# Pairs 4 and 5 of an attention and MLP kernel: output turned by transposing transfers, in a new recorded order

## The chip, the cores and the metric

The kernel runs on one core of one Trainium2 chip. The metric is the device time of one execution in microseconds, the median over runs. A core has five engines that run at the same time, each with its own queue of instructions: PE (TensorE, matmuls), DVE (VectorE), ACT (ScalarE), POOL (GpSimd) and SP (SyncE, which here only issues transfers). They wait for each other through semaphores.

## The reference

`q`, `k`, `v` have 4 batches, 8 heads, 768 positions and 64 values. Attention is block-sparse and causal: the mean of each block of 64 keys is compared with each query, and a query attends to the three blocks with the highest score and to its own block. The result, 3072 rows of 512 values, goes through an MLP.

```python
k_rep = k.reshape(B, H, n_blocks, block, D).mean(axis=3)
gate_scores = np.where(causal, q @ k_rep, -1e9)
sel = top3(gate_scores) | own_block
scores = np.where(sel & causal_positions, q @ k.T / 8, -1e9)
x = (softmax(scores) @ v)          # to 3072 x 512
out = gelu_tanh(x @ w_in) @ w_out  # 512 x 2048, 2048 x 512
```

## The kernel before

**Tiling.** The unit of attention is a pair of heads, `p` = 0 to 15; batch `b` is `p // 4` (`HP` = 4). For each pair, k and q are loaded and turned so that the head dimension lies on partitions, key block sums are taken, a gate matmul (L679) gives block scores, DVE picks the three best (L695 to L716), and the mask is turned on PE (L748, pairs below 8) or by a transposing transfer (L755). Then come the score matmuls (L855 for pairs 0 to 3, L1038 later), the exponential on ACT (L874, L1051), the causal cut on POOL (L900, L1065), the product with v (L923, L1077) and the normalisation on DVE (L941 and L942, L960 and L961), which writes `xn`. The MLP follows per batch: `x @ w_in` with gelu (L1114, L1126; a seven-product form at L1203) and the product with `w_out` (L1314, L1364, L1413), then stores.

**Loads.** `load_0` (L412) brings pair 0 in halves, k by SP and q by ACT (L420). `load` (L366) brings the rest by SP: plain for pairs 0 to 3 (L386), which PE then turns (L537 for k, L540 for q), and in pieces that DVE can turn in 32x32 blocks for pairs 4 to 15 (L392, L556). For pairs 0 and 1 (`KSUM`) the turning matmul of k also gives block sums. `load_w` (L442) brings `w_in` and `w_out` by POOL's queue (L452). Both kernels have these plain loads and key sums.

**From `xn` to the MLP's input `xT`.** `turn_out` (L964) turns the output of a pair. One way, `ot_e`, takes six 128x128 transposes on PE (L980) into a PSUM bank, and a copy on DVE or ACT (L359 and L355 in `copy`) to SBUF. The other, `ot_dma`, is one transposing transfer that SP issues (L985).

**What sets the order.** The builder makes some 1960 operations, each with an emitter. `Plan.run` emits them in a recorded global order, a list of numbers (`ORDER`), with a recorded choice of buffer for each (`BUFFER`) and of engine for operations that several engines can do (`ENGINE`). Each engine's queue is this order restricted to the engine. There is no scheduler at build time. The order before was recorded for the kernel before. Dummy matmuls (L1516) are part of it: they fill PE in the first microseconds and in places later; there are 34.

Of the kernel before, what the change touches and what calls it, by code (L numbers as in the profile page):

```python
# [227 lines left out]
def kernel(  # L228
# [16 lines left out]
    HP = H // 2  # L245
# [720 lines left out]
    def turn_out(p, norms, base):  # L966
        b, hp = divmod(p, HP)
# [610 lines left out]
    for p in range(HP, NPAIR):  # L1578
# [3 lines left out]
        b, hp = divmod(p, HP)  # L1582
# [36 lines left out]
```

## Time and profile before

| what | value |
|---|---|
| median of 3 runs | 251.66 us (251.35 to 251.76) |
| profiled execution, own time | 251.91 us |
| its span in the profile | 250.2 us (1.71 us lie around it) |
| busy: PE, DVE, ACT, POOL | 243.9, 188.3, 174.7, 85.2 us |
| L980 transposes on PE | 54, of 219 ns mean |
| L985 transposing transfers | 7 |

A row of a timeline gives the start, the length from first start to last end, the engine, the line, what is written and read, and how many instructions are run together in the row; in brackets stands the idle time before it and what ended it. Matmuls overlap in the pipeline: the time that one holds PE is the distance to the next start, not its length.

### The profile page before, as it was taken

The page shows a single profiled execution, that of the slowest core. Times are in us where ns is not written, and L with a number is a line of the kernel's source. Part 1 is how long each engine was busy: PE and PEld are TensorE (multiplying, and loading weights), DVE is VectorE, ACT ScalarE, POOL GpSimd, SP SyncE. Part 2 cuts the span into 40 slices and gives each one's busy share as a digit, 9 for nine tenths or more (in the row PEclk, how much of TensorE's full clock was granted, in tenths as well). Part 3 has the DMA queues.
Part 4 walks back from the last instruction along what each step waited for, and adds up shares of the span by engine and source line. Part 5 has one row for each costly group of instructions (what it writes and reads, how often), then busy time and mean ns, then how long its engine had stood idle before and what let it go on. Part 6 is the DMA issues. An engine that isn't in the chain of part 4 may idle for free.

```text
span 250.2 us, 6424 instructions
## 1 busy us (share of the span) xinstructions
PE 243.9 (97%) x2480; PEld 170.2 (68%) x2480; DVE 188.3 (75%) x541; ACT 174.7 (70%) x220; POOL 85.2 (34%) x166
## 2 busy tenths in 40 slices
PE   8899999999999999999999999999999999999993
PEld 6767676554556566665778887656877877666882
DVE  2799671034989999999999987998878584687953
ACT  0778896553699999668999873676999937657300
POOL 8853970001245655342156644500245600000000
PEclk9999999999999999999999999999999999999999
DMA  8999599998999998997999999550310350010023
GB/s 160 218 196 195 86 213 189 213 170 138 158 132 161 150 122 130 158 198 176 145 219 204 160 174 159 132 162 19 65 45 4 63 159 2 15 71 0 3 109 142
DMA packets 130927, 32.61 MB, mean 130 GB/s; under 512 B 124529, under 2 KB 126929, under 8 KB 130897
## 3 DMA queue, kind: packets, MB, share of 16 engines
q1 hardware_dynamic: 126160, 27.62, 64.1%
q0 software_dynamic: 3136, 4.19, 9.9%
q10 hardware_dynamic: 1600, 0.39, 0.8%
q8 instruction: 19, 0.31, 0.6%
q14 instruction: 12, 0.09, 0.1%
HBM read 27.26 MB, written 6.29 MB: 134 GB/s over the span
## 4 chain that ended last, share of the span: by engine, by line
PE 80%; DMA 8%; SPq 6%; POOL 3%; issue 1%; DVE 0%; POOLq 0%
PE wide L1114 24%; PE bank L1364 22%; PE wide L1038 11%; PE bank L1314 9%; PE bank L1077 6%; SPq L386 6%; PE wide L1203 6%; DMA w_out<-in_moe_w_out_dram 5%; DMA TS<-in_v_dram 2%; PE bank L679 2%; POOL ats L900 2%; DMA G<-in_q_dram 1%; PE bank L980 1%; POOL v L357 1%; POOL w_in L452 1%
## 5 line engine op out<-in xcount | busy, mean ns | idle before, releaser
L1114 PE MATMUL wide<-xT,w_in 128*128 128x384 f16 x416 | 74.6, 326 | 0.0
L1051 ACT ACTIVATE ats<-wide 128x896 f16<-128x896 f32 x72 | 62.1, 915 | 4.9 <-PE wide L1038 3.3
L1126 ACT ACTIVATE G<-wide 128x768 f16<-128x768 f32 x52 | 41.8, 809 | 29.3 <-PE wide L1114 29.1
L1114 PEld LDWEIGHTS <-w_in 128*128 128x128 f16 x416 | 39.8, 98 | 26.7 <-issue 1.3
L1065 POOL TENSOR_SCALAR_AFFINE_SELECT ats<-ats 128x256 f16<-128x256 f16 x72 | 32.0, 460 | 58.1 <-ACT ats L1051 57.7
L1038 PE MATMUL wide<-qT,kT 76*128 76x512 f16 (+3 forms) x192 | 39.0, 305 | 0.0
L556 DVE STREAM_TRANSPOSE s<-sd 128x768 f32<-128x768 f32 x24 | 23.1, 969 | 14.9 <-DMA sd<-in_k_dram 13.1
L1364 PE MATMUL bank<-w_out,G 128*128 128x256 f16 x216 | 32.9, 272 | 0.0
L1364 PEld LDWEIGHTS <-G 128*128 128x128 f16 x288 | 26.9, 98 | 5.8
L1413 DVE TENSOR_TENSOR osb<-bank,osb 128x512 f32<-128x512 f32 (+1 forms) x38 | 22.2, 594 | 9.1 <-PE bank L1364 8.4
L1314 PE MATMUL bank<-w_out,G 128*128 128x512 f16 x96 | 28.8, 379 | 0.1
L1077 PEld LDWEIGHTS <-ats 128*128 128x128 f16 x504 | 22.4, 98 | 3.8 <-POOL ats L1065 0.2
L1077 PE MATMUL bank<-v,ats 128*128 128x65 f16 x504 | 24.4, 194 | 0.0
L1038 PEld LDWEIGHTS <-kT 76*128 76x128 f16 x192 | 17.2, 97 | 9.8 <-issue 0.5
L874 ACT ACTIVATE ats<-wide 128x1024 f16<-128x1024 f32 (+3 forms) x24 | 20.9, 916 | 3.5 <-PE wide L855 3.3
L1364 PEld LDWEIGHTS <-XS 128*128 128x128 f16 x216 | 20.1, 97 | 4.2
L357 POOL CAST kT<-s 64x768 f16<-64x768 f32 x20 | 17.1, 867 | 16.5 <-DVE s L556 16.1
L1364 PE MATMUL bank<-TS,XS 128*128 128x256 f16 x144 | 22.3, 272 | 0.0
L357 POOL CAST v<-vsd 128x768 f16<-128x768 f32 x13 | 10.9, 840 | 30.8 <-DMA vsd<-in_v_dram 30.8
L961 DVE TENSOR_TENSOR xn<-bank,zr 128x384 f16<-128x384 f32 x24 | 13.4, 557 | 0.8
L711 DVE MAX8 sel<-sel 128x8 f32<-128x12 f32 x160 | 13.3, 157 | 0.6
L355 ACT CAST qT<-s 64x768 f16<-64x768 f32 x16 | 13.2, 828 | 0.2
(118 smaller groups left out, 347.3 us busy)
## 6 DMA issues: line engine op xcount, KB each, us to landing
out_dram<-osb SPq DMA_DIRECT2D x23, 256.0 KB
vsd<-in_v_dram SPq DMA_DIRECT2D x26, 192.0 KB
sd<-in_k_dram SPq DMA_DIRECT2D x48, 96.0 KB
sd<-in_q_dram SPq DMA_DIRECT2D x48, 96.0 KB
w_in<-in_moe_w_in_dram POOLq DMA_DIRECT2D x2, 1024.0 KB, 10.8
w_out<-in_moe_w_out_dram POOLq DMA_DIRECT2D x2, 1024.0 KB, 14.9
G<-in_q_dram SPq DMA_DIRECT2D x4, 192.0 KB
G<-in_k_dram SPq DMA_DIRECT2D x4, 192.0 KB
```

Of the source, the lines that this page charges most:

```text
L357: nc.gpsimd.tensor_copy(out=out, in_=in_)
L556: nc.vector.transpose(out=T[key + "T32", p], in_=T[key, p].rearrange("p t j -> p (t j)"))
L874: nc.scalar.activation(out=T["at", u][:, :, 0:n], in_=plan.buf[("st",) + u].rearrange("p (h w) -> p h w", h=2)[:, :, 0:n], func=AF.Exp, bi ...
L1038: nc.tensor.matmul(st[:, x:e], kT16[i][h][0:76, s0:s0 + 128], qT16[i][h][0:76, s0 + (x - cb):s0 + (e - cb)], start=True, stop=True)
L1051: nc.scalar.activation(out=T["at", u][:, 0:n], in_=plan.buf[("st",) + u][:, 0:n], func=AF.Exp, bias=0.0, scale=SCALE)
L1065: nc.gpsimd.affine_select(out=dg, in_=dg, compare_op=ALU.is_ge, fill=0.0, base=0, pattern=[[0, 2], [1, 128]], channel_multiplier=-1)
L1077: nc.tensor.matmul(pvv[:, qc, 0:65], at[:, cb + (qc - jc) * 128: cb + (qc - jc + 1) * 128], v16[i][:, jc, h, :], start=(gi == 0 and jc == ...
L1114: nc.tensor.matmul(hps[:, 512 * e:512 * e + HALF], w_in16[:, ci, (2 * j + e) * 128: (2 * j + e + 1) * 128], T["xT", b][:, ci, HALF * h:HAL ...
L1126: nc.scalar.activation(out=G[:, :, h, j, :], in_=plan.buf["hps", b, j, h].rearrange("p (e w) -> p e w", e=2)[:, :, 0:HALF], func=AF.Gelu_a ...
L1314: nc.tensor.matmul(plan.buf["ops", b, ti], G[:, f % 2, 2 * ti // NC, f // 2, ti % (NC // 2) * 128:ti % (NC // 2) * 128 + 128], w_out16[:, ...
L1364: nc.tensor.matmul(dst[:, HD * h:HD * h + HD], FACT[m][0][:, j, t * 128:(t + 1) * 128], FACT[m][1][:, j, :], start=(clear and j == 0), sto ...
L1413: nc.vector.tensor_tensor(out=dst(), in0=src(), in1=other(), op=ALU.add)
```

## The change

One condition, and all three recorded lists:

```diff
-        if p >= HP + 2 and hp != HP - 1:
+        if p >= HP and hp != HP - 1:
             go = add({SP: 1.3}, ot_dma, norms, -50)
...
-    0, 1890, 6, 9, 1891, 1892, 1893, 1894, 1895, 15, 12, 1896, 1897, 1898,
...
+    1, 1892, 2, 1893, 1894, 1895, 6, 15, 1896, 1897, 9, 1898, 1899, 1900,
+    195, 12, 1901, 1902, 1903, 1904, 1905, 1906, 1907, 62, 64, 71, 22, 72,
...
```

By the condition, pairs 4 and 5 now take `ot_dma` as pairs 6, 8, 9, 10, 12, 13 and 14 did. `ORDER`, `BUFFER` and `ENGINE` are new throughout. Counted in the programs: L980 goes from 54 matmuls (and as many weight loads) to 42, L985 from 7 transfers to 9, copies of `xT` on ACT from 3 to 1, on DVE they stay 7; the number of all other operations is the same. Some twenty casts and copies change their engine among DVE, ACT and POOL. At the start, the first two of ACT's four loads of pair 0's q are the second half of the positions, and the last two the first half; before it was the other way round. ACT's first table load moves from its first copy (L355) to L821, ahead of it. The last of the 34 dummy matmuls moves behind all other matmuls.

More of the change, by code (lines that the diff above doesn't have):

```diff
@@ L21 @@
 ORDER = [
[128 rows of a table removed]
-BUFFER = [
[23 rows of a table removed]
[128 rows of a table added]
+BUFFER = [
[23 rows of a table added]
 ENGINE = {
     "ACT": [
[4 rows of a table removed]
[4 rows of a table added]
     "POOL": [
-        586, 587, 646, 647, 707, 708, 972, 973, 1035, 1036, 1097, 1098,
-        1159, 1160, 1425, 1489, 1550, 1551, 1612, 1613]}
+        338, 587, 588, 648, 649, 709, 710, 974, 975, 1037, 1038, 1099, 1100,
+        1161, 1162, 1427, 1428, 1490, 1491, 1552, 1553, 1614, 1615]}
 class Op:
```

307 rows, old and new, of tables (BUFFER, ENGINE, ORDER) are left out of this document.

## The prediction

> **What bounds the kernel now.** I read the page first: busy times, the chain that ended last, and the granted clock.
>
> ```profile
> span 250.2 us, 6424 instructions
> PE 243.9 (97%) x2480; PEld 170.2 (68%) x2480; DVE 188.3 (75%) x541; ACT 174.7 (70%) x220; POOL 85.2 (34%) x166
> PEclk9999999999999999999999999999999999999999
> PE 80%; DMA 8%; SPq 6%; POOL 3%; issue 1%; DVE 0%; POOLq 0%
> ```
>
> TensorE is busy for 243.9 of 250.2 us, at full clock, and four fifths of the last chain are its own. Busy time is an average, so the next view is the table of stretches (columns: stretch, its length, then busy us of PE, weight loads, DVE, ACT, POOL).
>
> ```profile
> 0.00:10.00 10.00, 8.36 (x71) 6.31 (x73) 4.14 (x31) 3.65 (x7) 8.09 (x28) 1.00 1.02 182
> 10.00:20.00 10.00, 9.50 (x144) 6.84 (x140) 9.24 (x38) 7.62 (x12) 6.73 (x15) 1.00 1.17 206
> 20.00:30.00 10.00, 10.00 (x190) 7.54 (x184) 8.85 (x40) 9.45 (x12) 5.98 (x11) 1.00 0.68 118
> 30.00:40.00 10.00, 9.78 (x166) 7.56 (x163) 5.33 (x14) 8.07 (x11) 5.83 (x10) 1.00 1.13 211
> 40.00:50.00 10.00, 9.91 (x62) 5.70 (x61) 0.36 (x1) 5.14 (x7) 0.00 (x0) 1.00 1.31 200
> 90.00:100.00 10.00, 10.00 (x119) 6.47 (x116) 9.80 (x20) 9.83 (x13) 6.54 (x13) 1.00 1.00 121
> ```
>
> PE has nothing to fill but the first 10 us (1.64 idle), 0.5 in the next ten, 0.3 around 40. In 90 to 100 it never stops, though DVE and ACT are almost as full there: the late rivals lie in that stretch. What PE waited for most, over the whole span (us in total, times, longest):
>
> ```profile
> PE bank L1516 <- DVE bmask L284: 1.1, 1, 1.1
> PE bank L748 <- DVE madd L716: 0.5, 2, 0.3
> PE bank L540 <- DMA G<-in_q_dram: 0.4, 1, 0.4
> ```
>
> So the kernel is a stream of matmuls with a short ramp and a short tail. The time moves by what leaves that stream, and by what happens to the ramp.
>
> **The change, part by part.**
>
> *Twelve transposes leave PE.* Pairs 4 and 5 no longer go through six L980 transposes each.
>
> ```profile
> 96.41 0.50 PE L980 MATMUL bank<-ident,xn 128*128 128x128 f16 x6
> 96.74 0.38 PE L1314 MATMUL bank<-w_out,G 128*128 128x512 f16 x1
> ```
>
> Matmuls are pipelined, so I take starts, not busy times: six transposes hold the stream from 96.41 to 96.74, 0.33 us. Two pairs: **−0.67 us**, with PE full on both sides.
>
> *One filler leaves the path.* The program before has 34 dummy matmuls (L1516), the last of them in the tail's stream; the new order puts that one behind all real work. A filler in the stream costs what these starts are apart:
>
> ```profile
> 28.63 0.28 PE L1516 MATMUL bank<-XS 128*128 128x256 f16 x1
> 28.75 0.44 PE L748 MATMUL bank<-ident,madd 128*128 128x128 f16 x5
> ```
>
> **−0.12 us.**
>
> *Two copies leave DVE and ACT*, those that emptied the transposes' bank:
>
> ```profile
> 87.71 0.55 DVE L359 COPY xT<-bank 128x768 f16<-128x768 f16 x1
> 97.22 1.61 ACT L355 COPY xT<-bank 128x768 f16<-128x768 f16 x2
> ```
>
> That is 0.55 us of DVE and half of 1.61 of ACT. The planner also moves some twenty casts and copies between DVE, ACT and POOL. None of this is on the chain (DVE 0% of it), so I count zero; it is cover for the waits below. Its gain is bounded by zero, as PE has no idle time there to give back.
>
> *Two transposing transfers enter SP's queue* (L985, seven to nine).
>
> ```profile
> L985 SPq DMA_TRANSPOSE xT<-xn x7: 1211/1239/2051, 92.8 to 199.0; - x7
> 88.17 2.75 SPq L392 DMA_DIRECT2D sd<-in_q_dram  x4
> 92.80 2.05 SPq L985 DMA_TRANSPOSE xT<-xn  x1
> 94.90 1.71 SPq L392 DMA_DIRECT2D sd<-in_k_dram  x3
> 85.05 0.56 DVE L961 TENSOR_TENSOR xn<-bank,zr 128x384 f16<-128x384 f32 x1
> 95.87 0.49 PE L1114 MATMUL wide<-xT,w_in 128*128 128x384 f16 x2
> 98.05 2.11 PE L1114 MATMUL wide<-xT,w_in 128*128 128x384 f16 x12
> ```
>
> Each holds SP for about 1.24 us, 2.48 together. They stand ahead of pair 6's, where SP sat from 90.92 to 92.80 for pair 6's normalised output, 1.88 us. So about 0.6 us of later loads remains. Their first consumers (L1114 of batch 1, pair 4 and then 5) stand at 95.87 before, and in the order of the new program at about the same place. Pair 5's output is finished on DVE at 85.6 (85.05 + 0.56), pair 4's earlier; a transfer issued at 88 to 90 has six microseconds. Pair 6's own, whose issue ran from 92.80 to 94.85, feeds the third of the twelve L1114 from 98.05 (about 98.5) without a wait, so four suffice. Cost 0, and if the cover goes, PE stalls by the lateness (a rival below). The Trainium skill, page "VectorE: DVE Perf Modes", section "Rules for kernel authors", advises the opposite choice: TensorE for a 128×128 transpose whose result may land in PSUM, the crossbar DMA otherwise. By that rule the −0.67 would not be worth the latency; the rows here say that PE, not latency, is scarce in this stretch.
>
> *The order at the start is different, and that costs.* In the program before ACT issues pair 0's q as first half, then second half (L420). In the new program the second half is issued first, while PE's order still needs the first half first (turn k, turn q's first half, q's second half, filler, gate).
>
> ```profile
> 0.81 2.15 ACTq L420 DMA_DIRECT2D G<-in_q_dram  x4
> 0.81 2.86 DMA G<-in_q_dram
> 5.21 0.49 PE L540 MATMUL bank<-identk,G 128*128 128x128 f32 x3
> 6.35 0.32 PE L679 MATMUL bank<-s,ksb 128*32 128x64 f32 x8 [0.21 <-DVE s L359]
> 7.59 0.52 PE L540 MATMUL bank<-identk,G 128*128 128x128 f32 x3
> G<-in_q_dram ACTq DMA_DIRECT2D x4, 96.0 KB
> G<-in_k_dram SPq DMA_DIRECT2D x4, 96.0 KB
> ```
>
> The first issued transfer has landed by 3.67 (0.81 + 2.86). When the third and fourth do, no row says. Earliest: by the issue spacing alone (2.15 / 4), two places later, 3.67 + 1.1 = 4.8. Latest: 7.59, where the second half's turn ran without a wait. Between them: eight transfers of 96 KB, of k and q, run together. The first ten microseconds carry 1820 KB, all of it after some 2 us, so 228 KB per us while data flow; the six or seven left after 3.67 take 2.6 to 3.0 us: 6.3 to 6.7. I take 6.7, so the turn goes from 5.21 to about 6.8, **+1.6 us** at the first gate.
>
> How much reaches the end of the ramp? PE cannot catch up, since it is full from 20 us; but PE is not what sets the ramp. The gates' chain on DVE does, busy 9.24 and 8.85 of ten: 1.9 us of idle time, part of it waits that shift along with PE. The exponential's table load (1.28 us, in front of ACT's first copy before) comes earlier in the new order, and q's second half is there at once. Bounds: 0 (all regained in DVE's gaps) and 1.6 (none). I take the middle, **+0.8 us** at the first expert matmul. Part of that is given back in a known place:
>
> ```profile
> 33.54 12.43 DMA w_out<-in_moe_w_out_dram
> 38.95 1.79 PE L1114 MATMUL wide<-xT,w_in 128*128 128x384 f16 x10
> 40.57 0.33 PE L980 MATMUL bank<-ident,xn 128*128 128x128 f16 x3
> 40.87 5.05 PE L1114 MATMUL wide<-xT,w_in 128*128 128x384 f16 x30
> 46.01 0.38 PE L1314 MATMUL bank<-w_out,G 128*128 128x512 f16 x1
> ```
>
> w_out lands at 45.97. Ten L1114 matmuls take 1.62 in the stream (38.95 to 40.57), thirty so 4.86; L1314 came 5.14 after the first of the thirty: 0.28 of waiting, less a few hundredths, which a PE that arrives 0.8 late doesn't have: **−0.27**. Net start: +0.5, bounds −0.3 and +1.3.
>
> *The tail* (PE's last matmul, an addition on DVE, the last store) has the same shape and shifts as a whole.
>
> **Sum**: −0.67 − 0.12 + 0.8 − 0.27 = −0.26 us. The profiled execution took 251.91 us (span 250.2 and 1.71 around it), which gives 251.65; it stands 0.25 above the median of the runs shown, 251.66, so for a median I forecast **251.4 us**. That is 0.1% off; about 0.2%, or 0.5 us, is what a measurement can tell from no change here.
>
> **Rivals.**
>
> *The ramp absorbs the late half.* Then the stream keeps its −0.79, and the w_out wait, if it goes too, adds 0.27: −0.8 to −1.06, **250.8 us**. For it: DVE's 1.9 us of gaps, and the table load out of the way. Against it: the gates form one chain, in which those gaps are mostly waits for PE.
>
> *DVE waits for loads that the new transfers hold back (slower).* Place: the 32x32 transposes (L556) of pair 9's q at about 98 us, and pair 15's k at about 153 (places in the new order, counted in DVE's work).
>
> ```profile
> 108.76 0.98 DVE L556 STREAM_TRANSPOSE s<-sd 128x768 f32<-128x768 f32 x1 [0.29 <-DMA sd<-in_k_dram]
> ```
>
> Before, one load already came 0.29 late. SP is 0.6 later in the new order, so such a wait is 0.9, and two of them 1.8 at most. DVE has 0.2 us spare in 90 to 100, and its delay reaches PE through the next gate's mask. With one to one and a half of these on PE: −0.26 + 1.3 = +1.04, **252.7 us**. It decides once those loads are issued less than about 3.2 us ahead of DVE's turn. Against it: DVE has 0.55 us less to do, and PE holds other matmuls to run meanwhile.
>
> *The transposed outputs come late.* If pair 4's transfer is issued with pair 6's at 92.8 instead of at 88, it lands behind its consumer, and PE stalls by about 1 us: −0.26 + 1.0, 252.4. The new SP order speaks against it.
>
> *The clock falls in the ramp.* PE would stand for about 1.7 us before the late turn. The granted clock is 1.00 in the first row, which holds 1.64 us of idle time in all, so I expect no fall. If it fell, at the doubled spacing of the first fillers for some 1.7 us, that would be 253.1. The Trainium skill, page "TensorE: Matmul & The Clock Gate", Part 1, puts the fall behind an idle window of about 3.4 us; by it, too, this gap is too short.
>
> **How the numbers follow.** Forecast case 0.42 (−0.65 to +0.3 us), ramp absorbed 0.25, DVE late 0.22, outputs late 0.07, clock 0.04. Faster by over 0.2%: the second and 0.08 of the first, 0.33. Within: 0.34 of the first, 0.02 of the fourth, 0.36. Slower: the rest, 0.31. The range leaves out the clock, the outer half of the absorbed case and the dearest DVE waits: 250.7 to 252.8.
>
> **What would show it.** 42 L980 matmuls and nine L985 transfers, the first two at 88 to 91 us. The first q turn near 6.8 and the first L679 near 8.0 instead of 6.35. The first L1114 about 0.8 later than 35.85 and no gap before the first L1314. PE without waits from 50 on: if a wait for a mask or for xT stands there, the slower rivals hold; if the first L1114 starts no later than before, the faster one.

## The result and the profile after

The changed kernel takes **253.86 us** (253.27 to 254.32) against 251.71 us (251.35 to 251.98): 1.0085 times as long, interval 1.006 to 1.011, 2.15 us more. The prediction was 251.4 us, inside 250.7 to 252.8; the time lies above. The profiled execution of the changed kernel took 253.96 us.

First the page: busy times and the chain that ended last.

```profile
span 252.2 us, 6405 instructions
PE 245.9 (98%) x2468; PEld 171.3 (68%) x2468; DVE 191.9 (76%) x538; ACT 173.7 (69%) x218; POOL 88.3 (35%) x169
PEclk9999999999999999999999999999999999999999
PE 89%; DVE 4%; ACT 3%; DMA 2%; issue 1%; POOL 1%; ACTq 1%; DVEq 0%; POOLq 0%
```

There are twelve matmuls fewer, and yet PE is "busy" for 2 us longer. That is the first sign: matmuls that run slowly count as busy. The row of the granted clock shows 9 in every slice of both kernels and doesn't tell; the spacing of the matmuls does. PE at the start, the kernel before and then the changed one:

```profile
4.46 0.92 PE L537 MATMUL bank<-identk,G 128*128 128x130 f32 x6
...
6.60 0.94 PE L537 MATMUL bank<-identk,G 128*128 128x130 f32 x6
```

```profile
4.46 1.56 PE L537 MATMUL bank<-identk,G 128*128 128x130 f32 x6
6.75 1.51 PE L540 MATMUL bank<-identk,G 128*128 128x128 f32 x6 [0.73 <-DMA G<-in_q_dram]
...
8.40 0.44 PE L679 MATMUL bank<-s,ksb 128*32 128x64 f32 x8
8.77 1.61 PE L537 MATMUL bank<-identk,G 128*128 128x130 f32 x6
10.22 0.38 PE L1516 MATMUL bank<-XS 128*128 128x256 f16 x2
```

Six L537 take 0.92 us before and 1.56 to 1.61 after, at 4.46 and still at 8.77. The trace's record of the clock says the same: full from 4.62 us before, from 10.19 after. The first turn of q comes at 6.75 (I had said 6.8), the first gate at 8.40 instead of 6.35.

What that makes of the expert stage, in the timeline of PE: the first L1314 stood at 46.01 before, the first L1114 at 35.85.

```profile
35.85 1.78 PE L1114 MATMUL wide<-xT,w_in 128*128 128x384 f16 x10
```

After:

```profile
38.25 0.81 PE L1114 MATMUL wide<-xT,w_in 128*128 128x384 f16 x4
...
47.94 0.59 PE L1314 MATMUL bank<-w_out,G 128*128 128x512 f16 x2
...
245.82 2.57 PE L1364 MATMUL bank<-w_out,G 128*128 128x256 f16 x22
```

The last row ends at 248.39; before, the last run of L1364 ended at 246.30:

```profile
243.52 2.78 PE L1364 MATMUL bank<-w_out,G 128*128 128x256 f16 x24
```

So PE is 2.40 us late at the first L1114, 1.93 at the first L1314 and 2.09 at the end. Between the last two the stream is 0.79 us shorter (transposes and dummy), so 0.95 us of new waiting has come in there. These rows of PE show the larger part of it:

```profile
88.12 0.93 PE L1038 MATMUL wide<-qT,kT 76*128 76x512 f16 x6
89.15 0.45 PE L748 MATMUL bank<-ident,madd 128*128 128x128 f16 x5
...
97.05 0.59 PE L1077 MATMUL bank<-v,ats 128*128 128x65 f16 x14
97.86 0.61 PE L1077 MATMUL bank<-v,ats 128*128 128x65 f16 x14 [0.22 <-POOL ats L1065]
```

The mask of pair 7 starts 0.27 us after its place in the stream (six L1038 take 0.76), and two groups of v products are 0.81 us apart where fourteen of them take 0.43 in the stream: 0.38. The rest, some 0.3, are small gaps at a gate near 71 us and in the last batch.

The transfers hold nobody up. SP's queue:

```profile
L985 SPq DMA_TRANSPOSE xT<-xn x9: 1211/1214/2265, 89.1 to 201.2; - x9
```

```profile
89.08 3.46 SPq L985 DMA_TRANSPOSE xT<-xn  x2
```

Both are issued from 89.08 on. Two take 3.46 us where one holds SP for 1.21, so SP waits about 1 us between them: pair 5's output is ready on DVE at 91.31 here, not at 85.6 as in the kernel before. No L1114 waits for xT. There is no wait of DVE for q's or k's pieces from 60 us on either.

### The profile page after: what moved, and what is told of

It is laid out like the page before. It is cut to its first block, busy times and chain, and to the rows that moved or that the text cites. A ratio compares the mean times of both kernels' runs of the same rounds, so it can differ in the third digit from the quotient of the medians.

```text
span 252.2 us, 6405 instructions
## 1 busy us (share of the span) xinstructions
PE 245.9 (98%) x2468; PEld 171.3 (68%) x2468; DVE 191.9 (76%) x538; ACT 173.7 (69%) x218; POOL 88.3 (35%) x169
## 3 DMA queue, kind: packets, MB, share of 16 engines
q0 software_dynamic: 3136, 4.19, 10.3%
## 4 chain that ended last, share of the span: by engine, by line
PE 89%; DVE 4%; ACT 3%; DMA 2%; issue 1%; POOL 1%; ACTq 1%; DVEq 0%; POOLq 0%
PE wide L1114 27%; PE bank L1364 22%; PE wide L1038 10%; PE bank L1314 7%; PE wide L1203 6%; PE bank L1077 5%; PE wide L855 3%; ACT ats L1051 2%; PE bank L679 2%; PE bank L923 2%; DMA G<-in_q_dram 2%; PE bank L540 1%; PE bank L537 1%; PE bank L980 1%; PE bank L1516 1%; PE bank L748 1%
## 5 line engine op out<-in xcount | busy, mean ns | idle before, releaser
L1114 PE MATMUL wide<-xT,w_in 128*128 128x384 f16 x416 | 75.2, 326 | 0.0
L1051 ACT ACTIVATE ats<-wide 128x896 f16<-128x896 f32 x72 | 62.9, 915 | 4.8 <-PE wide L1038 3.2
L1114 PEld LDWEIGHTS <-w_in 128*128 128x128 f16 x416 | 39.9, 98 | 26.4 <-issue 1.0
L1038 PE MATMUL wide<-qT,kT 76*128 76x512 f16 (+3 forms) x192 | 39.1, 305 | 0.0
L357 POOL CAST kT<-s 64x768 f16<-64x768 f32 x23 | 19.6, 856 | 38.8 <-DVE s L556 38.1
L1364 PE MATMUL bank<-w_out,G 128*128 128x256 f16 x216 | 32.7, 272 | 0.0
L1364 PEld LDWEIGHTS <-G 128*128 128x128 f16 x288 | 27.0, 98 | 5.9
L1314 PE MATMUL bank<-w_out,G 128*128 128x512 f16 x96 | 28.7, 379 | 0.0
L1077 PE MATMUL bank<-v,ats 128*128 128x65 f16 x504 | 25.1, 194 | 0.2 <-POOL ats L1065 0.2
L1038 PEld LDWEIGHTS <-kT 76*128 76x128 f16 x192 | 17.0, 97 | 10.3 <-issue 0.5
L1364 PEld LDWEIGHTS <-XS 128*128 128x128 f16 x216 | 20.0, 97 | 5.4 <-issue 0.2
L1364 PE MATMUL bank<-TS,XS 128*128 128x256 f16 x144 | 23.6, 272 | 0.0
L357 POOL CAST v<-vsd 128x768 f16<-128x768 f32 x13 | 11.9, 919 | 15.7 <-issue 8.2
L355 ACT CAST qT<-s 64x768 f16<-64x768 f32 x18 | 14.9, 827 | 0.3
```

The lines of the kernel that those rows point to most:

```text
L357: nc.gpsimd.tensor_copy(out=out, in_=in_)
L1038: nc.tensor.matmul(st[:, x:e], kT16[i][h][0:76, s0:s0 + 128], qT16[i][h][0:76, s0 + (x - cb):s0 + (e - cb)], start=True, stop=True)
L1051: nc.scalar.activation(out=T["at", u][:, 0:n], in_=plan.buf[("st",) + u][:, 0:n], func=AF.Exp, bias=0.0, scale=SCALE)
L1077: nc.tensor.matmul(pvv[:, qc, 0:65], at[:, cb + (qc - jc) * 128: cb + (qc - jc + 1) * 128], v16[i][:, jc, h, :], start=(gi == 0 and jc == ...
L1114: nc.tensor.matmul(hps[:, 512 * e:512 * e + HALF], w_in16[:, ci, (2 * j + e) * 128: (2 * j + e + 1) * 128], T["xT", b][:, ci, HALF * h:HAL ...
L1314: nc.tensor.matmul(plan.buf["ops", b, ti], G[:, f % 2, 2 * ti // NC, f // 2, ti % (NC // 2) * 128:ti % (NC // 2) * 128 + 128], w_out16[:, ...
```

## The experiments

The theory after the result had two parts: the late half of q at the start, with the half-speed clock behind it, costs about 1.9 us, and the new order's later waits cost 1 us, while the condition alone gains. The rivals: the first gate's own steps on DVE and PE are the start's loss whatever q does; the transfers cost by themselves. Orders are lists of operation numbers; where two orders are joined, the diff says so in words.

**q_first.** The two halves of q change places in the new order.

```diff
-    1, 1892, 2, 1893, 1894, 1895, 6, 15, 1896, 1897, 9, 1898, 1899, 1900,
+    1, 1892, 2, 1893, 1894, 1895, 6, 9, 1896, 1897, 15, 1898, 1899, 1900,
```

> The changed kernel with one edit: ACT issues the first half of pair 0's q before the second again. Theory 1 (the late half, and the half-speed PE clock that stays because PE stands still for it, cost the ramp its 1.9 us): first L540 near 5.2 us, matmuls 0.11 us apart from about 5 us on, first L1114 near 36.2, time 251.8. Theory 2 (what DVE and PE now do ahead of the first selection is the larger cost, whatever q does): the first L748 still 1 us or more later than before, time 252.8 or more.

253.26 us (251.89 to 254.27), 1.0053 (1.0031 to 1.0075). PE's timeline:

```profile
5.31 0.49 PE L540 MATMUL bank<-identk,G 128*128 128x128 f32 x3
6.77 0.52 PE L540 MATMUL bank<-identk,G 128*128 128x128 f32 x3 [0.96 <-DMA G<-in_q_dram]
...
7.32 0.32 PE L679 MATMUL bank<-s,ksb 128*32 128x64 f32 x8
...
36.57 0.81 PE L1114 MATMUL wide<-xT,w_in 128*128 128x384 f16 x4
...
47.18 0.59 PE L1314 MATMUL bank<-w_out,G 128*128 128x512 f16 x2 [0.62 <-DMA w_out<-in_moe_w_out_dram]
```

The first half is turned at 5.31, but PE's order has the second half's turn ahead of the gate, and that half lands at 6.77. So the gate needs both, in whichever order they come. The clock is full from 4.8 us in this execution, ahead of PE's first work that the edit moves (5.31), so that part isn't the edit's. The first L1114 is 1.68 us earlier than in the changed kernel, and then w_out takes back 0.62: the new order issues it 1.0 us ahead of the first L1114 (35.57 here), where the order before does so 2.3 us ahead (33.54). The profiled execution is the slowest of these runs (254.27). The signs are split: the first L1114 comes near what theory 1 said (36.2), but the first mask is 1.18 us later than before (10.11 against 8.93) and the time is above 252.8, as theory 2 said. The swap alone doesn't undo the start's loss.

**gap_filled.** Eight dummies in PE's pause.

```diff
-    62, 64, 71, 22,
+    62, 64, 1926, 1927, 1928, 1929, 1930, 1931, 1932, 1933, 71, 22,
```

> The changed kernel with eight more dummy matmuls (L1516) between the turn of k's first half and that of q's, so that PE is busy while it waits; q is as late as in the changed kernel. If the half-speed clock is a part of the loss: the turns from 6.8 us on are 0.11 us apart instead of 0.21, and 0.8 to 1.3 us come back: 252.8. If only the late data counts: 253.9, or up to 0.3 more by the dummies themselves.

253.64 us (252.42 to 255.44), 1.0078 (1.0047 to 1.0109). PE in the profiled execution (253.44):

```profile
4.49 0.91 PE L537 MATMUL bank<-identk,G 128*128 128x130 f32 x6
...
36.54 0.81 PE L1114 MATMUL wide<-xT,w_in 128*128 128x384 f16 x4
```

The six turns of q take 0.85 us instead of 1.51, and the first L1114 is 1.71 us earlier than in the changed kernel, with q as late as ever (6.71). But the clock had risen by 4.49, ahead of the eight dummies at 5.23, so they didn't cause it, and whether filling the pause helps isn't shown. Nor are the 1.71 us the price of half speed alone: new_ramp2, below, starts as the changed kernel does, also has a full clock, and gains 0.54. The times show no gain: the interval overlaps that of the changed kernel.

**old_q_late.** The halves change places in the order *before*: the late half alone.

```diff
-    0, 1890, 6, 9, 1891, 1892, 1893, 1894, 1895, 15, 12,
+    0, 1890, 6, 15, 1891, 1892, 1893, 1894, 1895, 9, 12,
```

> The kernel before with one edit: ACT issues the second half of pair 0's q ahead of the first. Theory 1 (the late half delays the first gate by 1.6 us, and PE's pause can keep its clock at half speed): first L540 at 6.8 us, first L1114 0.5 us (full clock) to 2.2 us (half speed until 10 us) later than 35.85, time 252.2 to 253.5. Theory 2 (the ramp absorbs a late half, and only the rest of the new order costs): 251.8.

252.98 us (252.35 to 254.75) against 251.96, 1.004 (1.0009 to 1.007).

```profile
7.01 0.52 PE L540 MATMUL bank<-identk,G 128*128 128x128 f32 x3 [1.19 <-DMA G<-in_q_dram]
...
8.18 0.32 PE L679 MATMUL bank<-s,ksb 128*32 128x64 f32 x8 [0.21 <-DVE s L359]
...
37.38 1.78 PE L1114 MATMUL wide<-xT,w_in 128*128 128x384 f16 x10
...
47.14 0.38 PE L1314 MATMUL bank<-w_out,G 128*128 128x512 f16 x1
```

The clock is full here from 5.4 us on, and still the gate's 1.83 us arrive at the first L1114 as 1.53 and at the first L1314 as 1.13. Theory 1 holds: in this execution the ramp gives back 0.3 of the late half's 1.83 us. Smaller delays shrink more: cond_late, best_b, cond_only, v_early, mid_fix and old_ramp start in the order of before, and as their clock rises later, the first gate comes at 6.78 to 7.32, up to 0.97 late; the first L1114 stands at 35.74 to 36.24, at most 0.39 late. In the time the late half costs 1.0 us (0.2 to 1.8 by the interval).

**no_warm.** The kernel before without the sixteen dummies ahead of the first turn.

```diff
-    1890, 1891, 1892, 1893, 1894, 1895, 1896, 1897, 1898, 1899, 1900,
-    1901, 1902, 1903, 1904, 1905,
```

> The kernel before, without the sixteen dummy matmuls ahead of the first turn, so that PE's first matmul comes at 4.46 us and its clock is still at half speed in the first gates. If half speed in the ramp costs as much as the changed kernel's profile suggests: matmuls 0.21 us apart until 8 to 10 us, first L1114 1 to 1.7 us later than 35.85, time 252.7 to 253.3. If the ramp hides it: 251.7 to 252.0.

252.70 us (252.2 to 253.67) against 251.84, 1.0029 (1.0015 to 1.0043).

```profile
4.28 1.64 PE L537 MATMUL bank<-identk,G 128*128 128x130 f32 x6 [4.28 <-DMA G<-in_k_dram]
...
7.71 1.67 PE L537 MATMUL bank<-identk,G 128*128 128x130 f32 x6
...
10.40 0.49 PE L540 MATMUL bank<-identk,G 128*128 128x128 f32 x3
...
37.90 1.78 PE L1114 MATMUL wide<-xT,w_in 128*128 128x384 f16 x10
```

Half speed until about 10 us, as in the changed kernel, with data as early as before: 2.05 us at the first L1114 in the profiled execution (253.67, the slowest of its runs), 0.7 to 0.9 in the time. Half speed in the ramp has a cost of its own, without a late half.

**cond_only.** The condition alone, in the order before; both transfers stand where pair 4's copy stood.

```diff
-    ot_e(4), otc_e(4), ot_e(5), otc_e(5)
+    ot_dma(4), ot_dma(5)
```

> The condition of the change alone: pairs 4 and 5 through SP's transposing transfers, in the order of the kernel before, with the two transfers where DVE copied pair 4's output. If the transfers are hidden: PE's stream is 0.67 us shorter, 251.0. If they hold back loads or land late: 251.7 or more, with a wait of DVE's L556 or of L1114.

253.84 us (253.75 to 256.33), 1.0114 (1.0079 to 1.015): the second of the two cases. SP, DVE and PE:

```profile
80.66 6.20 SPq L985 DMA_TRANSPOSE xT<-xn  x2
86.91 1.71 SPq L392 DMA_DIRECT2D sd<-in_k_dram  x3
```

```profile
91.33 0.98 DVE L556 STREAM_TRANSPOSE s<-sd 128x768 f32<-128x768 f32 x1 [0.96 <-DMA sd<-in_k_dram]
...
95.99 0.98 DVE L556 STREAM_TRANSPOSE s<-sd 128x768 f32<-128x768 f32 x1 [1.31 <-DMA sd<-in_k_dram]
```

```profile
99.40 0.51 PE L980 MATMUL bank<-ident,xn 128*128 128x128 f16 x6 [1.72 <-DVE xn L961]
```

SP reaches the pair at 80.66 and waits in pair 5's transfer until that pair is normalised, near 85.6, with the loads of k behind it. DVE waits 2.3 us for them, and PE 1.72 for DVE. This is my slower rival, dearer than its price (2.05 us in the time where it had 1.04), but made by the place and not by the transfer.

**cond_late, cond_late_b.** The same, with the two transfers behind the first piece of pair 9's q, where SP arrives at 88.

```diff
     first(q, 9),
+    ot_dma(4), ot_dma(5),
```

> The condition of the change in the order of the kernel before, as in cond_only, but the two transfers stand behind the loads that SP issues before 89 us, so that SP does not wait for pair 5's output with loads behind it. If cond_only lost its time to that wait alone: no wait of PE for xn at 99 us, DVE's L556 waits at most 0.3 us, 0.67 us less than before: 251.1. If the transfers cost by themselves (landing late, slower loads): 251.8 or more.

251.36 us (250.9 to 252.35) against 251.84, 0.9982 (0.9968 to 0.9997). The second set of runs of the same kernel, cond_late_b:

> The kernel of the run cond_late again: 0.3 to 0.5 us below before, and at most 0.3 above best_b.

252.10 us (250.72 to 253.06) against 251.84, 0.9997 (0.9974 to 1.0019). One set says faster, the other can't tell. In the first one's profile (252.35, its slowest run) SP holds nobody up, and a new wait of PE appears:

```profile
88.09 2.65 SPq L985 DMA_TRANSPOSE xT<-xn  x2
```

```profile
88.04 0.55 PE L1038 MATMUL wide<-qT,kT 76*128 76x512 f16 x3
88.70 0.45 PE L748 MATMUL bank<-ident,madd 128*128 128x128 f16 x5
```

```profile
88.36 0.28 DVE L716 SCALAR_TENSOR_TENSOR madd<-sel,ownm 128x120 f16<-128x120 f32 x1
```

Three L1038 take 0.38 us, so PE could have begun the mask at 88.42. DVE's selection ends at 88.64. Pair 4's six transposes (0.33 us) had stood ahead of this mask; without them PE comes earlier and waits 0.28 for DVE.

**best, best_b.** cond_late with that mask behind one more L1314, and the last dummy at the end.

```diff
-    676, 719, 669, 960, 703, 681, 522, 665,
+    676, 669, 960, 703, 681, 522, 719, 665,
...
-    1735, 1925, 1777,
+    1735, 1777,
...
-    1890, 1850]
+    1890, 1850, 1925]
```

> cond_late with two moves on PE: the mask of pair 7 (L748, where PE waited 0.28 us in cond_late) stands behind one more L1314 of batch 0, and the last dummy matmul stands behind all other work. If half of the saved transposes was given back at that mask: 0.2 us of it returns, and 0.11 for the dummy: 251.05 against 251.36 of cond_late. If DVE's selection is what paces PE there, the wait moves on to the next score product and the time stays within 0.1 of cond_late less the dummy: 251.25.

251.62 us (250.88 to 253.14) against 251.96, 0.9977 (0.9949 to 1.0004). The second set:

> The kernel of the run best again: the condition in the old order, with the mask and the dummy moved. 251.3 to 251.6, 0.3 to 0.5 us below before on the same chip. If the earlier gain was the spread of those runs: within 0.1 of before.

251.30 us (250.9 to 252.41) against 251.84, **0.9972 (0.9951 to 0.9993)**: faster than both kernels. Of the two sets only this one's interval lies clear of 1. The mask hardly waits in its profile, 0.06 us behind an L1314 that takes 0.22 in the stream:

```profile
86.72 0.55 PE L1038 MATMUL wide<-qT,kT 76*128 76x512 f16 x3
87.11 0.38 PE L1314 MATMUL bank<-w_out,G 128*128 128x512 f16 x1
87.39 0.45 PE L748 MATMUL bank<-ident,madd 128*128 128x128 f16 x5
```

**old_ramp.** The order before up to the first L1114, the new order behind it.

```diff
-    (new order up to the first L1114)
+    (order before, up to the first L1114)
     (new order from there on)
```

> The changed kernel's order from the first L1114 on, behind the order of the kernel before up to there. If the whole loss is the ramp's: first L1114 at 35.9, and 0.8 us less than before by the shorter stream, 250.9. If the new order also loses some 0.8 us by itself between 60 and 240 us (the waits at 89 and 98 us in the changed kernel): 251.7.

253.52 us (253.23 to 253.87), 1.0069 (1.0052 to 1.0087). The joint has a wait of its own (L1114 for ACT's gelu, 0.9 us), so this doesn't price the rest alone. But the mask of pair 7 (0.30) and the last v products of pair 7 (0.38) wait here as in the changed kernel, with an early ramp: these waits belong to the new order.

**new_ramp2.** The other way round: the new order up to the first L1114, then cond_late's.

```diff
-    (order of cond_late up to the first L1114)
+    (new order up to the first L1114)
     (order of cond_late from there on)
```

> The order of the changed kernel up to the first L1114, then cond_late's. If the ramp of the new order costs about 1.9 us and its rest the other part: 251.36 + 1.9 = 253.3, less where an execution has full clock early (then 252.0). If the ramp's loss is regained later: 251.5.

254.0 us (252.25 to 254.83), 1.0034 (0.9999 to 1.0069), in two groups, near 252.4 and near 254.3. Above cond_late by some 2.6 us at the median, with a wait at the joint (0.9) as in old_ramp. Up to the joint this is the changed kernel's program, and in its profiled execution (253.98, of the slower group) the clock was full from 5.6 us on:

```profile
6.85 0.85 PE L540 MATMUL bank<-identk,G 128*128 128x128 f32 x6 [0.94 <-DMA G<-in_q_dram]
...
37.71 0.81 PE L1114 MATMUL wide<-xT,w_in 128*128 128x384 f16 x4
```

So with the same start, a late q and a full clock the first L1114 is only 0.54 us earlier than in the changed kernel (37.71 against 38.25), and an execution with a full clock can fall in the slower group; what divides the groups isn't shown. Against gap_filled's 36.54 this execution is 1.17 late with a clock as full. Most of that stands in single steps of DVE on the gates' chain: a cast of 0.95 us at 8.00 (0.36 there), an L716 of 0.78 at 21.88 and an L702 of 0.58 at 28.24 (0.28 each there). What lengthens such a step in one execution wasn't tested.

**pe45_new.** The new order with pairs 4 and 5 on PE, that is, without the change.

```diff
-    ot_dma(4), ot_dma(5)
+    ot_e(4), otc_e(4), ot_e(5), otc_e(5)
```

> The new order without the change: pairs 4 and 5 are turned by PE again (L980, twelve matmuls, and two copies), all else as in the changed kernel. If the loss is the new order's alone and the transfers save their 0.67 us: 254.5. If the transfers are what the changed kernel pays for: 252.5 or less.

256.29 us (254.92 to 256.96), 1.0161 (1.0136 to 1.0186). More than the 0.67 us of transposes: the two copies that I had to place made v products wait for DVE and POOL (0.5 and 0.9). So the transfers aren't what the changed kernel pays for; what they save isn't separated from the place of the two copies.

**old_start, start_fixed.** Two repairs of the start in the new order. The first takes the order before up to the first whole score product; the second only puts the first gate's steps back into their sequence.

```diff
-    (new order up to pair 0's first whole score product)
+    (order before up to there)
     (new order from there on)
```

> The changed kernel with the first operations, up to the first whole score product of pair 0, in the order of the kernel before: q's first half first, its second half turned behind the gate, no casts of DVE ahead of the selection. If the order of the start makes the ramp late: first L748 near 9, first L855 near 9.8, first L1114 near 36.0 instead of 38.25, and, as w_out is issued later in this order, 0.5 to 1 us of waiting before the first L1314; time 252.8. If the ramp stays late: 253.8.

```diff
-    6, 15, 1896, 1897, 9,
+    6, 9, 1896, 1897, 15,
...
-    72, 73, 74, 1908, 0, 82, 23, 75, 18, 66, 63, 76, 1909, 1910, 100, 1911, 68, 19,
+    72, 1908, 0, 23, 75, 18, 66, 73, 74, 76, 77, 68, 82, 63, 1909, 1910, 100, 1911, 19,
...
-    99, 77, 84,
+    99, 84,
```

> The changed kernel with the first gate's steps in their old sequence, nothing else: q's first half is issued first, its second half is turned behind the gate and behind k's, and DVE selects before it casts and before it sums k's second half. If these steps are the start's whole loss: first L679 near 6.4 to 7.1, first L748 near 9, first L1114 near 36.2 instead of 38.25, then up to 1 us of waiting for w_out, which this order issues later; time 252.8. If the later work of DVE in the new order is late in any case: first L1114 above 37, 253.4 or more.

old_start: 253.37 us (252.82 to 254.71), 1.0046 (1.0028 to 1.0063), first mask at 9.26, but the first L1114 at 37.36. start_fixed: 254.84 us (253.97 to 255.97), 1.0116 (1.0084 to 1.0149), worse than the changed kernel. Its first gate is early and its mask isn't:

```profile
6.22 0.32 PE L679 MATMUL bank<-s,ksb 128*32 128x64 f32 x8 [0.54 <-DVE s L359]
...
8.30 0.27 PE L1516 MATMUL bank<-XS 128*128 128x256 f16 x1 [0.57 <-ACT s L355]
9.46 0.27 PE L1516 MATMUL bank<-XS 128*128 128x256 f16 x1 [0.89 <-DVE XS L359]
...
11.13 0.28 PE L748 MATMUL bank<-ident,madd 128*128 128x128 f16 x2
```

The dummies wait for banks that casts on ACT and DVE still read, since the recorded choice of banks belongs to the other sequence. Neither repair mends the start, and what its DVE part costs by itself stays open.

**mid_fix, v_early.** Edits of old_ramp at pair 7: first POOL's casts of pair 8's k behind pair 7's causal cuts, and the mask behind one more L1314; then also POOL's cast of pair 7's v ahead of the cuts.

```diff
-    680, 719, 519, 677,
+    680, 519, 719, 677,
...
-    1035, 975, 579, 732, 628, 528, 675, 974, 529,
+    1035, 579, 732, 628, 528, 675, 529,
...
-    743, 740,
+    743, 974, 975, 740,
```

> old_ramp (here with the transfers of the changed kernel's order, as before) with two edits around 88 to 98 us: POOL casts pair 8's k behind pair 7's last causal cut instead of ahead of it, and pair 7's mask stands behind one more L1314 on PE. If POOL's casts, moved there from DVE by the new assignment, are what pair 7's last v products waited for (0.38 us), and the mask takes 0.25: 252.9 against 253.52 of old_ramp, no wait of L1077 near 96 us. If ACT's exponentials set that place: 253.4.

```diff
-    1085, 734, 726, 533, 706, 727,
+    1085, 706, 734, 726, 533, 727,
```

> mid_fix with one more edit: POOL casts pair 7's v ahead of pair 7's causal cuts (there it waited 2.25 us for ACT) instead of between them. If the cast, which holds POOL for 0.8 us in front of four cuts, makes the last v products wait: no wait of L1077 at 96.5 us, 0.38 less: 252.45 against 252.85. If ACT's last exponential sets it: the wait stays.

252.85 us (252.35 to 253.98), 1.0017 (0.999 to 1.0045), and 252.69 us (252.4 to 253.35), 1.0032 (1.0016 to 1.0048). The mask's wait falls to 0.07, but the v products still wait 0.37 to 0.38 in both. So mid_fix meets the 252.9 that was said for it without the cause that was said. POOL in v_early:

```profile
95.16 1.72 POOL L1065 TENSOR_SCALAR_AFFINE_SELECT ats<-ats 128x256 f16<-128x256 f16 x3 [0.85 <-ACT ats L1051]
```

POOL now sits idle for ACT. So my theory of POOL's casts falls, and ACT's exponentials, back to back there, are what is left; that is read from the rows and wasn't undone.

## Why the prediction was wrong, point by point

The forecast puts PE's end at −0.26 us; in the profiles it is at +2.09. Of these 2.35 us, 1.40 are there at the first L1314 (1.93 instead of +0.53) and 0.95 come in behind it.

- **The twelve transposes, −0.67: right as a length of stream, too large as a gain.** The condition alone in a fitting place gives 0.48 us in one set of runs and nothing certain in the other, since 0.28 of it turns into a wait at the next mask. With that mask moved and the dummy gone it is 0.3 to 0.5 us.
- **The dummy, −0.12, and the transfers at 0: not contradicted.** Pair 5's output comes later than the row of before said (91.31, not 85.6), but the first L1114 that can use it stands at 98.31, so it still has nearly six microseconds, and nobody waits.
- **The start, +0.8 taken as "the middle" between 0 and 1.6: the term that failed.** The delay itself was right (6.75 against 6.8). How much of it reaches the experts was not: old_q_late shows 1.53 at the first L1114 for the late half alone, in one execution. The argument from DVE's 1.9 us of gaps didn't hold. The waits long enough to be listed among them, 0.3 us for the gate's scores and 0.3 for the mask, are both waits for PE, as the text itself held against the rival; the rest are gaps under 0.2 us. In the changed kernel the gate waits for both halves as well, which I had listed and not priced.
- **The clock, a rival with 0.04, is in the profile**, though the clock didn't fall: it never rose before 10.19. I looked for a fall in the row of the granted clock, which reads full in both kernels, and not at the spacing, 0.21 against 0.11 us, which had been in the trace of before. Together with the late half it makes the larger part of the 2.40 us at the first L1114; its share isn't settled (full clock goes with 0.54 us less in new_ramp2 and with 1.71 less in gap_filled), and neither is how many of the other executions had it.
- **The wait for w_out, −0.27: gone, but not by the reason given.** The sum let PE arrive late at a landing that stays at 45.97. The new order issues w_out at 37.24 instead of 33.54, and it lands 10.6 us later, near 47.8; the first L1314 follows at 47.94. That nothing was left of the wait is luck: an earlier ramp would have met it, as in q_first (0.62).
- **"The moved casts are cover, so zero": wrong by about 0.95 us** behind the first L1314. I priced how much work each engine has and not where it stands. From 70 to 100 us of the changed kernel DVE is busy for about 9.5 of each ten and ACT for 8.2 to 9.9, so a new sequence easily makes new waits for PE. Both copies of xT left ACT (three to one), not one ACT and one DVE.
- **The slower rival, DVE waiting for loads**, isn't in the changed kernel. cond_only shows that it exists, with 2 us, when a transfer waits at the head of SP's queue.

## What to carry to other kernels

Price a searched order by the chain at its start and by what each engine does just ahead of every hand-over; total work per engine says nothing of it. Take a delay on an unbroken chain at nearly its full length (1.53 of 1.83 us here), however many gaps the engines show, unless a row names other work that fills them. One profile is one execution: the same start was 0.54 us apart at its end in two of them, so compare several before a difference of that size is put down to an edit. A transfer that takes work off the bound engine gains only up to the next wait for another engine, and it must be issued when its input is ready, or it holds the queue behind it.

## What the runs showed of the hardware that was not expected

**When PE's clock rises differs from execution to execution, and a pause can put it off.** All profiles but no_warm's begin PE with the same dummies at 1.07 us, 0.21 us apart. In the eleven that don't wait for a late half of q the clock rose (the spacing halved) between 3.7 and 6.8 us. In the other six PE waits for it, for 0.4 to 1.2 us, until 6.7 to 7.0. In four of them (q_first, gap_filled, old_q_late, new_ramp2) the clock had risen before that pause, at 4.2 to 5.6, and it stayed up through it. In the changed kernel and pe45_new it had not, and it rose only at 10.2 and 10.3, 3.4 and 3.7 us after the turn. So a late half doesn't by itself keep the clock at half speed; it does when the pause comes before the rise. The Trainium skill, page "TensorE: Matmul & The Clock Gate", Part 1, states about 3.4 us of sustained activity in a window that runs freely; the trace agrees with a free window (the stretches at full clock last 242.35, 245.76 or 249.17 us, steps of 3.41), but in start_fixed the clock rose 2.7 us after PE's first matmul.

**A causal cut on POOL can take five times as long beside DVE's sums.** At 124 us in q_first two cuts took 3.01 us, the second alone 2.21; in the changed kernel two took 1.60, and the median of one is 0.41. POOL, q_first and then the changed kernel:

```profile
124.42 3.01 POOL L1065 TENSOR_SCALAR_AFFINE_SELECT ats<-ats 128x256 f16<-128x256 f16 x2 [5.87 <-ACT ats L1051]
```

```profile
125.17 1.60 POOL L1065 TENSOR_SCALAR_AFFINE_SELECT ats<-ats 128x256 f16<-128x256 f16 x2 [5.73 <-ACT ats L1051]
```

In q_first DVE ran L1301 (sums of two tensors) back to back beside the second cut, and PE waited 0.61 us for it. In the changed kernel DVE ran the same three beside its second cut, which took 0.80:

```profile
125.21 1.49 DVE L1301 TENSOR_TENSOR XS<-G,XS 128x768 f16<-128x768 f16 x3
```

```profile
125.96 1.69 DVE L1301 TENSOR_TENSOR XS<-G,XS 128x768 f16<-128x768 f16 x3
```

The Trainium skill, page "SBUF — State Buffer", section "Who interferes with whom", says that a DVE instruction with two SBUF inputs contends with a GpSimd instruction that reads SBUF; the rows agree that one side is slower than alone, the cut in q_first and the sums (1.69 against 1.49) in the changed kernel, and no run here separates the two or shows what decides between them. PE's wait stands in some profiles of the new order and not in others, which is one source of their spread; the rest of that spread stays open.
